# A gated linear-attention layer and its GEGLU block: first-unit PSUM copies on VectorE, constant matmuls in the ramp, and the residual added on VectorE in place of an accumulating DMA

## The chip, the core and the metric

One core of a Trainium2 chip runs the kernel. The metric is device time in microseconds (us) of one execution. The engines are TensorE (PE; its weight loads are PEld), VectorE (DVE), ScalarE (ACT), GpSimd (POOL) and SyncE (SP). SP and POOL issue the DMAs. Each engine takes its instructions in the order in which the compiler laid them down, and waits on semaphores for the others.

## What is computed

The reference has two parts. The first is a recurrence over 768 steps for 4 batches and 8 heads of width 48, with a complex decay per step and channel:

```
mag = sqrt(a_re^2 + a_im^2); scale = min(mag, 0.999) / (mag + 1e-6)
S[t] = (scale * (a_re + i a_im))[t] * S[t-1] + k[t] v[t]^T      (S complex, 48 x 48)
y[t] = q[t] . Re S[t]
```

The second takes x, the 3072 x 384 array of all y, through a gated block and adds x:

```
out = x + sigmoid(x @ w_res) * ((gelu(x @ w_gate) * (x @ w_val)) @ w_out)
```

Inputs and output are float32; d_ff is 1536.

## The kernel before, in words

**Tiling.** The 3072 tokens are cut into 12 groups (g0 to g11) of 256 tokens, two chunks (c = 0, 1) of 128 each; three groups make a batch. The groups are bundled in seven units: [0], [1,2], [3,4], ..., [9,10], [11]. The recurrence is done as chunked attention: the logarithm and the angle of the decay are summed along a chunk by matmuls with triangular matrices; exp and sin/cos of the sums scale q and k, and masked products of the two with v give y; a state per head goes from group to group.

**Two kinds of stage alternate.** `phase_x(u)` is the short one. It holds the output projection of unit u-1 (`op_step`, L459 to L472), the second half of unit u's attention, the decays of unit u+1 (`cs_l`, `carry`, `cs_t`, `p2_sin`) and the first steps of the decays of unit u+2 (`p1_steps`, `p1_arctan`). `phase_y(u)` is the long one: the gate and value matmuls of unit u (`gv_step`, `gp` and `vp`), the products `qE`, `Q`, `kE`, `K` of unit u+1 (`products`), and the first half of its attention. `weave` gives every list of steps a begin and an end as fractions of the stage and sorts all steps by them; the framework then schedules the instructions of each engine, with the attention marked as high priority. ACT changes its function table between stages (L477), and `tab` holds the order of the ACT functions fixed.

**Names that recur.** L124 is the line of all ACT functions that go through `act`: `ar` (Ln and arctan work in place on `ar` and `ai`), `s`, `E` and `Ei` (exp of the sums), `CS` (sine and cosine), `h` (gelu), `sg` (tanh). On DVE: `ai` L189 (the ratio of the decay's parts), `ar` L197 and L198 (log of the size, and its limit), `r` L243, `fg` L244 and `fg` L246 (the angle's fraction, and its absolute value for the cosine), `Q` and `K` L321, `atm` L359 (the mask), `h` L446, `ot` L466. On PE: `csl` L212 and `cst` L236, L238 (the sums, float32), `tp` L346 and L349 (transposes of Q and K), `at` L356, `dk` L386 (the state), `y` L394 and L396, `tpx` L424 (transposes of x), `gp` L439, `vp` L443, `rp` L455, `op` L463.

**Copies out of PSUM in attention.** In each half-head group `grp` the transposed Q goes to SBUF on ACT (L351) and the transposed K on DVE (L352). `x` leaves PSUM on ACT (L399). `xT` leaves it on ACT for even chunks (L428) and on DVE for odd ones (L430). PSUM is fully given out: four buffers for `csl`, `cst`, `ms`, `tpx`, `gp`, `vp`, `rp` and `op` in turn (psM), and one each for `tp`, `at`, `y` and `dk`.

**Residual.** For all units but the last, `ot` is stored by an SP DMA (L470), and a POOL DMA then adds the bfloat16 `x` to the stored rows in memory (L472, `accum_op`). It waits for the store. For the last unit DVE adds `x` to `ot` (L469) before the store. POOL also issues the loads of `v` and of the weights, and the small transfers through DRAM (`dm`, `m`, L262 and L265) that turn a row of decays into a column; DVE multiplies these in `M` L282 and L283.

**The ramp.** In the first stages, before unit 0 has its gate matmuls, the first group's decays, its attention and the decays of g1 to g4 follow each other with little beside them; the loads are in flight at the same time. The stage `phase_x(0)` has its own `weave` (L545 to L549).

Of the kernel before, what the change touches and what calls it, by code (L numbers as in the profile page):

```python
# [28 lines left out]
def kernel(  # L29
# [173 lines left out]
        act(out=T["th", g], in_=T["th", g], func=AF.Arctan)  # L203


    def cs_l(g, c):
        if c == 0:
            T["E", g] = pE.tile([128, W], FP, tag="E", name="E")
            T["Ei", g] = pE.tile([128, W], FP, tag="Ei", name="Ei")
        sl = slice(c * DM, (c + 1) * DM)  # L210
        cs = psM.tile([128, DM], FP, tag="mm", padded_shape=[128, 512], name="csl")
        nc.tensor.matmul(out=cs, lhsT=lmat[c], rhs=T["lm", g][:, sl], start=True, stop=True)  # L212

        def ex():
            act(out=T["E", g][:, sl], in_=cs, func=AF.Exp)
            act(out=T["Ei", g][:, sl], in_=cs, func=AF.Exp, scale=-1.0)
        return ex
# [11 lines left out]
    def cs_t(g, c):  # L229
        s = g % NS  # L230
        th = T["th", g]
        if c == 0:
            T["fg", g] = pE.tile([128, C * H, 2, D], FP, tag="fg", name="fg")
        sl = slice(c * DM, (c + 1) * DM)
        cs = psM.tile([128, DM], FP, tag="mm", padded_shape=[128, 512], name="cst")
        nc.tensor.matmul(out=cs, lhsT=tmat[c], rhs=th[:, sl], start=True, stop=(s == 0))  # L236
        if s > 0:
            nc.tensor.matmul(out=cs, lhsT=ones2pi, rhs=T["P", g], start=False, stop=True)  # L238
        cs3 = cs.rearrange("p (h d) -> p h d", h=H)
        fg = T["fg", g]  # L240
        hs = slice(c * H, (c + 1) * H)
        r = pS.tile([128, H, D], FP, tag="r", name="r")
        nc.vector.tensor_scalar(out=r, in0=cs3, scalar1=MAGIC, scalar2=MAGIC, op0=OP.add, op1=OP.subtract)  # L243
        nc.vector.tensor_tensor(out=fg[:, hs, 1, :], in0=cs3, in1=r, op=OP.subtract)  # L244
        if c == C - 1:
            nc.vector.tensor_scalar(out=fg[:, :, 0, :].bitcast(mybir.dt.int32), in0=fg[:, :, 1, :].bitcast(mybir.dt.int32),  # L246
                                    scalar1=0x7FFFFFFF, scalar2=None, op0=OP.bitwise_and)

    def p2_sin(g):
        T["CS", g] = pQ.tile([128, C * H, 2, D], BF, tag="CS", name="CS")  # L250
# [76 lines left out]
    def attention(g, c):  # L327
        s = g % NS
        first = s == 0 and c == 0
        st = {}  # L330

        def Q(x):
            return T["Q", g][:, x].rearrange("p u d -> p (u d)")

        def K(x):
            return T["K", g][:, x].rearrange("p u d -> p (u d)")

        def V(h):
            return T["v", g][:, c, h]

        def grp(hg):
            def a():
                tp = psT.tile([128, 1024], BF, tag="tp", name="tp")
                for j in range(4):
                    x = c * H + hg * 4 + j
                    nc.tensor.transpose(out=tp[0:DD, j * 128:j * 128 + 128], in_=Q(x), identity=ident)  # L346
                for j in range(4):
                    x = c * H + hg * 4 + j
                    nc.tensor.transpose(out=tp[0:DD, 512 + j * 128:640 + j * 128], in_=K(x), identity=ident)  # L349
                qk = sqp.tile([128, 1024], BF, tag="qk", name="qk")  # L350
                nc.scalar.copy(out=qk[0:DD, 0:512], in_=tp[0:DD, 0:512])  # L351
                nc.vector.tensor_copy(out=qk[0:DD, 512:1024], in_=tp[0:DD, 512:1024])  # L352
                st["qk", hg] = qk
                at = psA.tile([128, 4, 128], FP, tag="at", name="at")
                for j in range(4):
                    nc.tensor.matmul(out=at[:, j], lhsT=qk[0:DD, 512 + j * 128:640 + j * 128],  # L356
                                     rhs=qk[0:DD, j * 128:j * 128 + 128], start=True, stop=True)
                atm = sqp.tile([128, 4, 128], BF, tag="atm", name="atm")
                nc.vector.tensor_tensor(out=atm, in0=at, in1=mask4, op=OP.mult)  # L359
                st["atm", hg] = atm  # L360
            return a

        def enter():
            if s == 0 or c > 0:
                return
            d = T["dk", g - 1][0:DD].rearrange("p (h d) -> p h d", h=H)
            Mb = T["M", g][0:DD].rearrange("p (h u) -> p h u", u=1).to_broadcast([DD, H, D])
            G = stt.tile([128, H, D], FP, tag="G", name="G")
            if s == 1:
                nc.vector.tensor_tensor(out=G[0:DD], in0=d, in1=Mb, op=OP.mult)  # L370
            else:
                nc.vector.tensor_tensor(out=G[0:DD], in0=d, in1=T["G"][0:DD], op=OP.add)
                nc.vector.tensor_tensor(out=G[0:DD], in0=G[0:DD], in1=Mb, op=OP.mult)
            Gb = stt.tile([128, H, D], BF, tag="Gb", name="Gb")
            nc.vector.tensor_copy(out=Gb[0:DD], in_=G[0:DD])
            T["G"] = G
            T["Gbf"] = Gb

        def dk():
            if s == NS - 1 and c == C - 1:  # L380
                return
            if c == 0:
                T["dk", g] = psD.tile([128, DM], FP, tag="dk", padded_shape=[128, 512], name="dk")
            d = T["dk", g]
            for h in range(H):
                nc.tensor.matmul(out=d[0:DD, h * D:(h + 1) * D], lhsT=K(c * H + h), rhs=V(h),  # L386
                                 start=(c == 0 and h == 0), stop=(h == H - 1), skip_group_check=True)

        def yy():
            y = psY.tile([128, DM], FP, tag="y", padded_shape=[128, 512], name="y")  # L390
            for h in range(H):
                ys = y[:, h * D:(h + 1) * D]
                hg, j = divmod(h, 4)
                nc.tensor.matmul(out=ys, lhsT=st["atm", hg][:, j], rhs=V(h), start=True, stop=first)  # L394
                if not first:
                    nc.tensor.matmul(out=ys, lhsT=st["qk", hg][0:DD, j * 128:j * 128 + 128],  # L396
                                     rhs=T["Gbf"][0:DD, h], start=False, stop=True)
            x = xp.tile([128, DM], BF, tag="x", name="x")
            nc.scalar.copy(out=x, in_=y)  # L399
            T["x", g * C + c] = x  # L400
            if c == 0:
                d = T["dk", g][0:DD].rearrange("p (h d) -> p h d", h=H)
                Gb = stt.tile([128, H, D], BF, tag="Gb", name="Gb")
                if s == 0:
                    nc.vector.tensor_copy(out=Gb[0:DD], in_=d)
                else:
                    nc.vector.tensor_tensor(out=Gb[0:DD], in0=d, in1=T["G"][0:DD], op=OP.add)
                T["Gbf"] = Gb

        def hi(f):  # L410
            def w():
                with tc.high_priority():
                    f()
            return w
        return [hi(f) for f in (enter, grp(0), dk, grp(1), yy)]


    def xt_step(u, jj):
# [5 lines left out]
            nc.tensor.transpose(out=tpx[:, f * 128:(f + 1) * 128], in_=x[:, f * 128:(f + 1) * 128], identity=ident)  # L424
        dst = T["xT", u][:, :, jj * 128:(jj + 1) * 128]
        src = tpx.rearrange("p (f t) -> p f t", f=KD)
        if jj % 2 == 0:
            nc.scalar.copy(out=dst, in_=src)  # L428
        else:
            nc.vector.tensor_copy(out=dst, in_=src)  # L430
# [28 lines left out]
    def op_step(u, jj):  # L459
        h2 = T["h2", u]  # L460
        ps = psM.tile([128, DM], FP, tag="mm", padded_shape=[128, 512], name="op")
        for ffi in range(KF):
            nc.tensor.matmul(out=ps, lhsT=h2[:, ffi, jj * 128:(jj + 1) * 128], rhs=wo[:, ffi, :],  # L463
                             start=(ffi == 0), stop=(ffi == KF - 1))
        ot = ob.tile([128, DM], FP, tag="ot", name="ot")
        nc.vector.scalar_tensor_tensor(out=ot, in0=T["sg", u][:, jj], scalar=1.0, in1=ps, op0=OP.add, op1=OP.mult)  # L466
        t0 = token(u, jj) * 128
        if u == NU - 1:
            nc.vector.tensor_tensor(out=ot, in0=ot, in1=T["x", token(u, jj)], op=OP.add)  # L469
        nc.sync.dma_start(out=out[t0:t0 + 128, :], in_=ot)  # L470
        if u < NU - 1:
            nc.gpsimd.dma_start(out=out[t0:t0 + 128, :], in_=T["x", token(u, jj)], accum_op=OP.add)  # L472


    def table(nm):
# [32 lines left out]
    def phase_x(u):  # L508
# [34 lines left out]
        if u == 0:  # L543
            sm = [[call(sums, g) for g in gg if g % NS > 0] for gg in (g1, g2)]
            weave((0.0, 0.25, zip_steps([p1(g) for g in g1])), (0.26, 0.3, csls), (0.31, 0.32, sm[0]), (0.35, 0.45, exs),  # L545
                  (0.4, 0.64, zip_steps([p1(g) for g in g2])), (0.641, 0.642, dec3), (0.645, 0.65, atn[:1]),
                  (0.65, 0.66, [call(p1_arctan, g) for g in g1]), (0.67, 0.85, cst), (0.75, 0.8, atn[1:]),
                  (0.9, 0.95, sin), (0.96, 0.97, sm[1]), (0.0, 0.5, att))
            return  # L549
        if u == 1:  # L550
# [80 lines left out]
```

## Time and profile before

| | |
|---|---|
| median of 3 runs | 324.42 us (323.83 to 324.49) |
| the profiled execution | 324.49 us, span 322.4 us |
| mean granted TensorE clock | 0.949 |
| PE busy | 272.1 us (84%) in 2200 matmuls |
| DVE busy | 234.8 us (73%) in 431 instructions |
| ACT busy | 209.8 us (65%) in 353 |
| POOL busy | 80.5 us (25%) in 115 |
| 22 accumulating DMAs, POOL's part | 20.4 us |
| the chain that ended last | PE 56%, SP's queue 12%, ACT 11%, DMA 9%, DVE 6% |

The span runs from the first to the last instruction of the profiled execution. The shares of busy time are means over stages of different kinds, so they don't say what a change in one stage is worth. The granted clock is given as a share of full speed; a PE that waits is also "busy" in a pipelined matmul, so its share is an upper bound. The chain is followed back from the last instruction, at each step to what released it.

### The profile page before, as it was taken

How to read it: one execution, taken by the hardware profiler on the slowest of the kernel's cores; microseconds unless marked ns; L12 is line 12 of the kernel's file. 1: busy time of each engine (PE TensorE's matmuls, PEld its weight loads, DVE VectorE, ACT ScalarE, POOL GpSimd, SP SyncE). 2: the span in 40 equal slices, each digit the busy share in tenths (PEclk: the TensorE clock that was granted, in tenths of full speed). 3: DMA queues.
4: the chain of work that ended last, by engine and by line, in shares of the span. 5: the costliest groups of instructions: out<-in, count | busy, mean ns of one | idle time of the engine just before them, and what ended most of it. 6: DMA issues, size and time to landing. Idle time of an engine off the chain costs nothing.

```text
span 322.4 us, 5853 instructions
## 1 busy us (share of the span) xinstructions
PE 272.1 (84%) x2200; PEld 170.5 (53%) x2200; DVE 234.8 (73%) x431; ACT 209.8 (65%) x353; POOL 80.5 (25%) x115
## 2 busy tenths in 40 slices
PE   0337927789887999789997999998999999899994
PEld 0116624677543666445664556554656655555682
DVE  2446769968499995599982999974899837864352
ACT  4549684646998557977568976569665683656150
POOL 1206522022040370259020572000630003200220
PEclk9995676959999999999999999999999999999998
DMA  8999999989999995396850595000360003600441
GB/s 159 218 183 181 182 169 165 185 174 180 187 179 186 223 160 33 76 197 113 122 36 2 107 121 95 2 0 3 75 122 3 2 0 76 122 2 0 107 91 50
DMA packets 137755, 34.55 MB, mean 107 GB/s; under 512 B 126848, under 2 KB 137728, under 8 KB 137728
## 3 DMA queue, kind: packets, MB, share of 16 engines
q1 hardware_dynamic: 103296, 23.60, 36.8%
q0 software_dynamic: 34432, 10.59, 31.2%
q8 instruction: 17, 0.28, 0.3%
q14 instruction: 10, 0.08, 0.1%
HBM read 31.31 MB, written 9.07 MB: 125 GB/s over the span
## 4 chain that ended last, share of the span: by engine, by line
PE 56%; SPq 12%; ACT 11%; DMA 9%; DVE 6%; issue 3%; POOL 1%; ACTq 0%; DVEq 0%; POOLq 0%
PE vp L443 14%; PE gp L439 13%; SPq L136 6%; SPq L144 6%; PE op L463 6%; DMA k<-in_k_dram 4%; PE rp L455 3%; PE tp L349 3%; PE tp L346 3%; PE at L356 3%; ACT L477 3%; DMA m<-dm 3%; ACT s L124 3%; PE cst L236 2%; PE y L394 2%
## 5 line engine op out<-in xcount | busy, mean ns | idle before, releaser
L124 ACT ACTIVATE h<-gp 128x512 bf16<-128x512 f32 (+1 forms) x84 | 44.5, 536 | 38.4 <-PE gp L439 37.9
L439 PE MATMUL gp<-xT,wg 128*128 128x512 bf16 (+1 forms) x252 | 65.4, 353 | 3.4 <-ACT h L124 2.0
L443 PE MATMUL vp<-xT,wv 128*128 128x512 bf16 (+1 forms) x252 | 66.6, 353 | 0.0
L446 DVE SCALAR_TENSOR_TENSOR h<-h,vp 128x512 bf16<-128x512 bf16 (+1 forms) x84 | 49.8, 603 | 16.4 <-PE vp L443 12.0
L463 PE MATMUL op<-wo,h 128*128 128x384 bf16 x288 | 50.2, 326 | 8.1 <-ACT Ei L124 5.9
L463 PEld LDWEIGHTS <-h 128*128 128x128 bf16 x288 | 27.8, 98 | 28.7 <-issue 11.3
L351 ACT COPY qk<-tp 96x512 bf16<-96x512 bf16 x48 | 27.9, 580 | 17.1 <-PE tp L349 7.9
L359 DVE TENSOR_TENSOR atm<-at,mask 128x512 bf16<-128x512 f32 x48 | 32.9, 686 | 8.2 <-PE at L356 7.8
L472 POOL DMA_DIRECT2D out_dram<-x x22 | 20.4, 947 | 54.4 <-DMA out_dram<-ot 43.1
L439 PEld LDWEIGHTS <-wg 128*128 128x128 bf16 x252 | 23.7, 99 | 17.9 <-issue 4.2
L443 PEld LDWEIGHTS <-wv 128*128 128x128 bf16 x252 | 23.8, 99 | 13.3
L189 DVE TENSOR_TENSOR ai<-s,ai 128x768 f32<-128x768 f32 x12 | 11.1, 955 | 23.6 <-ACT s L124 23.6
L477 ACT ACT_TABLE_LOAD x21 | 26.9, 1283 | 1.1 <-PEq L615 0.7
L346 PE MATMUL tp<-ident,Q 128*96 128x128 bf16 x192 | 20.1, 231 | 6.9 <-DVE Q L321 6.2
L346 PEld LDWEIGHTS <-Q 128*96 128x96 bf16 x192 | 17.4, 130 | 15.3 <-DVE Q L321 10.0
L124 ACT ACTIVATE CS<-fg,hpi 128x768 bf16<-128x768 f32 x12 | 11.2, 935 | 20.8 <-DVE fg L246 20.7
L150 POOL DMA_DIRECT2D v<-in_v_dram x24 | 21.9, 932 | 4.2 <-DMA v<-in_v_dram 1.3
L349 PE MATMUL tp<-ident,K 128*96 128x128 bf16 x192 | 22.3, 235 | 0.0
L236 PE MATMUL cst<-ai,lt0b 128*128 128x384 f32 x24 | 11.8, 577 | 11.7 <-ACT ai L124 11.0
L352 DVE COPY qk<-tp 96x512 bf16<-96x512 bf16 x48 | 19.8, 413 | 2.3 <-ACT qk L351 1.7
L212 PE MATMUL csl<-ar,lt0a 128*128 128x384 f32 x24 | 11.4, 562 | 10.8 <-DMA ar<-in_a_re_dram 10.8
L466 DVE SCALAR_TENSOR_TENSOR ot<-sg,op 128x384 f32<-128x384 f32 x24 | 13.1, 547 | 10.1 <-PE op L463 10.1
(85 smaller groups left out, 522.0 us busy)
## 6 DMA issues: line engine op xcount, KB each, us to landing
ar<-in_a_re_dram SPq DMA_DIRECT2D x24, 192.0 KB, 4.7
ai<-in_a_im_dram SPq DMA_DIRECT2D x24, 192.0 KB, 4.1
q<-in_q_dram SPq DMA_DIRECT2D x24, 192.0 KB, 3.8
k<-in_k_dram SPq DMA_DIRECT2D x24, 192.0 KB, 3.7
out_dram<-ot SPq DMA_DIRECT2D x24, 192.0 KB, 2.5
out_dram<-x POOLq DMA_DIRECT2D x22, 192.0 KB, 3.7
v<-in_v_dram POOLq DMA_DIRECT2D x24, 96.0 KB, 5.0
wg<-in_moe_w_gate_dram POOLq DMA_DIRECT2D x4, 288.0 KB, 11.4
```

The lines of the kernel that those rows point to most:

```text
L124: tab(nc.scalar.activation(**kw))
L150: nc.gpsimd.dma_start(out=t[:, c], in_=rows(v, g, c))
L346: nc.tensor.transpose(out=tp[0:DD, j * 128:j * 128 + 128], in_=Q(x), identity=ident)
L349: nc.tensor.transpose(out=tp[0:DD, 512 + j * 128:640 + j * 128], in_=K(x), identity=ident)
L351: nc.scalar.copy(out=qk[0:DD, 0:512], in_=tp[0:DD, 0:512])
L359: nc.vector.tensor_tensor(out=atm, in0=at, in1=mask4, op=OP.mult)
L439: nc.tensor.matmul(out=gp, lhsT=wg[:, fi, ffi * 128:(ffi + 1) * 128], rhs=xT[:, fi, :], start=(fi == 0), stop=(fi == KD - 1))
L443: nc.tensor.matmul(out=vp, lhsT=wv[:, fi, ffi * 128:(ffi + 1) * 128], rhs=xT[:, fi, :], start=(fi == 0), stop=(fi == KD - 1))
L446: nc.vector.scalar_tensor_tensor(out=h2[:, ffi, :], in0=h2[:, ffi, :], scalar=0.5, in1=vp, op0=OP.mult, op1=OP.mult)
L463: nc.tensor.matmul(out=ps, lhsT=h2[:, ffi, jj * 128:(jj + 1) * 128], rhs=wo[:, ffi, :], start=(ffi == 0), stop=(ffi == KF - 1))
L472: nc.gpsimd.dma_start(out=out[t0:t0 + 128, :], in_=T["x", token(u, jj)], accum_op=OP.add)
L477: tab(nc.scalar.preload_act_table_set(nm))
```

## The change

There are six edits.

1. `warm(out, n)` is new: n matmuls of constant operands (the identity and the mask) into a PSUM tile that the real matmuls overwrite afterwards. It is called ahead of the first `csl` (10), of the first `cst` of g0 (12) and of g1 (16), of each `at` of g0 (2, four times) and of each `y` of g0 (2, twice).
2. For g0, the copies `qk` (L351) and `x` (L399) go to DVE.
3. For unit 0, both `xT` copies go to DVE (in the kernel before, one of the two).
4. The absolute value in `fg` is made from -f and f by a maximum, in float32, and no longer by a mask on the bits.
5. The arctans of g3 and g4 in `phase_x(0)` move from 0.75-0.8 to 0.98-0.99 of the stage, behind the sines.
6. The residual is added by DVE for every unit, before the store; the accumulating DMA is gone.

```diff
+    def warm(out, n):
+
+        for _ in range(n):
+            nc.tensor.matmul(out=out, lhsT=ident, rhs=mask4.rearrange("p j t -> p (j t)")[:, 0:out.shape[1]],
+                             start=True, stop=True)
+
...
         cs = psM.tile([128, DM], FP, tag="mm", padded_shape=[128, 512], name="csl")
+        if g <= FIRST and c == 0:
+            warm(cs, 10)
...
         cs = psM.tile([128, DM], FP, tag="mm", padded_shape=[128, 512], name="cst")
+        if g <= FIRST + 1 and c == 0:
+            warm(cs, 12 if g <= FIRST else 16)
...
-            nc.vector.tensor_scalar(out=fg[:, :, 0, :].bitcast(mybir.dt.int32), in0=fg[:, :, 1, :].bitcast(mybir.dt.int32),
-                                    scalar1=0x7FFFFFFF, scalar2=None, op0=OP.bitwise_and)
+            nc.vector.scalar_tensor_tensor(out=fg[:, :, 0, :], in0=fg[:, :, 1, :], scalar=-1.0, in1=fg[:, :, 1, :],
+                                           op0=OP.mult, op1=OP.max)
...
-                nc.scalar.copy(out=qk[0:DD, 0:512], in_=tp[0:DD, 0:512])
+                (nc.vector.tensor_copy if g <= FIRST else nc.scalar.copy)(out=qk[0:DD, 0:512], in_=tp[0:DD, 0:512])
...
+                if g <= FIRST:
+                    warm(at.rearrange("p j t -> p (j t)"), 2)
...
+            if g <= FIRST:
+                warm(y, 2)
...
-            nc.scalar.copy(out=x, in_=y)
+            (nc.vector.tensor_copy if g <= FIRST else nc.scalar.copy)(out=x, in_=y)
...
-        if jj % 2 == 0:
+        if jj % 2 == 0 and u > 0:
             nc.scalar.copy(out=dst, in_=src)
...
+        nc.vector.tensor_tensor(out=ot, in0=ot, in1=T["x", token(u, jj)], op=OP.add)
         t0 = token(u, jj) * 128
-        if u == NU - 1:
-            nc.vector.tensor_tensor(out=ot, in0=ot, in1=T["x", token(u, jj)], op=OP.add)
         nc.sync.dma_start(out=out[t0:t0 + 128, :], in_=ot)
-        if u < NU - 1:
-            nc.gpsimd.dma_start(out=out[t0:t0 + 128, :], in_=T["x", token(u, jj)], accum_op=OP.add)
...
-                  (0.65, 0.66, [call(p1_arctan, g) for g in g1]), (0.67, 0.85, cst), (0.75, 0.8, atn[1:]),
+                  (0.65, 0.66, [call(p1_arctan, g) for g in g1]), (0.67, 0.85, cst), (0.98, 0.99, atn[1:]),
```

## The prediction, made before the changed kernel was run

> **What bounds the kernel now.** I read the page's slices first, for the granted clock, then the stages one by one. (Line numbers are those of the kernel before; g0 to g11 are the groups.)
>
> ```profile
> PEclk9995676959999999999999999999999999999998
> ```
>
> A slice is 8.1 us. TensorE runs at reduced clock only between 24 and 72 us: the ramp, from the first unit's attention to the second unit's. Next, busy time by stage; the columns are length, PE, PEld, DVE, ACT, POOL (each with its instructions), granted clock, DMA share and GB/s.
>
> ```profile
> 24.00:38.00 14.00, 10.80 (x88) 8.71 (x89) 10.38 (x17) 10.85 (x18) 8.43 (x11) 0.53 1.16 186
> 44.50:54.20 9.70, 3.96 (x6) 2.14 (x7) 8.02 (x14) 7.68 (x11) 2.77 (x4) 0.50 1.31 179
> 64.80:71.20 6.40, 5.75 (x44) 4.79 (x44) 4.12 (x10) 2.61 (x7) 1.23 (x3) 0.50 0.84 164
> ```
> ```profile
> 173.00:192.00 19.00, 16.54 (x80) 9.22 (x78) 13.68 (x27) 16.57 (x27) 10.05 (x15) 1.00 0.52 80
> 192.00:219.00 27.00, 26.87 (x275) 16.40 (x275) 23.96 (x44) 17.32 (x32) 2.47 (x3) 1.00 0.25 40
> ```
>
> The last two rows are one period of the steady part. The long stage (192 to 219) is bound by PE: busy 26.87 of 27. In the short stage (173 to 192), where the decays of the next unit are made, PE has 2.5 us of idle time. Its DVE looks lightly loaded, but in the timeline it waits 5.1 us for ACT's squares first; from 177.59 to the end it has work without a gap, except one:
>
> ```profile
> DVE M L282 <- DMA m<-dm: 0.7, 1, 0.7
> ```
>
> So each short stage ends through DVE's queue: the second `fg` L246, then ACT's sines and gelu table, then `h`, or L246, then `Q` L321 and the transposes. Work put on DVE between `ai` L189 and `Q` there moves the start of the long stage. That holds in five stages: 83 to 102, 127 to 148, 173 to 192, 219 to 236, 262 to 276. Durations (the last three columns are count, busy us, mean ns, then idle before):
>
> ```profile
> L359 DVE TENSOR_TENSOR atm<-at,mask 128x512 bf16<-128x512 f32 x48 | 32.9, 686 | 8.2 <-PE at L356 7.8
> L352 DVE COPY qk<-tp 96x512 bf16<-96x512 bf16 x48 | 19.8, 413 | 2.3 <-ACT qk L351 1.7
> L197 DVE SCALAR_TENSOR_TENSOR ar<-s,ar 128x768 f32<-128x768 f32 x12 | 11.3, 951 | 3.3 <-ACT s L124 3.3
> L246 DVE TENSOR_SCALAR fg<-fg 128x768 int32<-128x768 int32 x12 | 6.7, 558 | 0.0
> L469 DVE TENSOR_TENSOR ot<-ot,x 128x384 f32<-128x384 f32 x2 | 1.1, 558 | 0.1
> ```
>
> **Residual add.** 22 accumulating DMAs leave the POOL queue (L472, 947 ns each); 22 adds like L469 enter DVE. Back to back, start to start, DVE spends 0.47 us on an operation of this shape (`ot` at 139.94, the next at 140.41), so 10.3 us in all. SP's store waits for the add, and the loads queued behind it on SP start 0.5 us later; DMA share is 0.15 to 0.6 there, so I cost this at nothing. `x` comes free earlier. On POOL the decay transfers `m<-dm` no longer stand behind an accumulation: at most the three waits for `m` (0.7, 1.0, 1.6 us) go, and they cover adds instead.
>
> **fg.** The and-mask (558 ns) becomes a two-operand form; nearest row L197, same shape, 951 ns. So 0.4 us dearer, twelve times, always between `cst` and the sine.
>
> **The five short stages.** I laid the compiled DVE order of the new kernel on the start-to-start times of the old.
> Stage at 83: before the second L246 come one new add, the second `ot` (formerly behind it, 0.47) and two dearer L246 (0.8): L246 ends 1.66 late, `h` and `Q` 1.7.
> Stage at 127: two adds and 0.8, less an operation that moved: `h` 1.5, `Q` 1.1 late; PE had no slack at 148. Taken 1.3.
> Stage at 173: three adds, an `ot` and 0.8, less two `M` operations and their 0.7 wait: `h` 1.2, `Q` 2.3. Taken 1.5.
> Stage at 219: `kE` moves behind the wait for `m` (1.0), which hides it: `h` 0.45, `Q` 1.4. Taken 0.8.
> Stage at 262: the 1.6 wait hides two adds; one dearer L246: 0.4.
> Sum 5.7 us. Bounds: nothing, if PE's idle time (2 to 3 us a stage) takes it all; 10.3 + 4.7 = 15 with every added operation on the path. In the last stage the adds lie beside PE (DVE waits 1.3 to 1.5 us for each `op` there): nothing.
>
> **Ramp, start.** PE gets 14 constant matmuls ahead of the first `csl`. They need the masks (DVE, until 8.23). At half clock a 384-column matmul takes 0.32 us (three of 256 take 0.64 at 67.1), at full clock 0.163 (twelve take 1.95): 4.7 us at half, so they end at about 12.9, where `csl` began at 10.81. `csl` and `cst` then ran at half speed (1.44 from one group to the next); at full speed they take 0.65. `E` of the second half comes 0.7 late if the clock has risen, 1.9 if not; a fast `cst` gives 0.7 back; the dearer L246 takes 0.4. By the first of two rows on the rise (next paragraph) it comes 3.9 us after 8.2, ahead of `csl`. Taken: `Q` +0.3 (bounds -0.4 and +2.3).
>
> The rows for the clock's rise: work resumes at 50.24, and full clock stands from 54.15, 3.9 us later; but between 24 and 37, 77% busy, it did not rise for 13 us. [...]
>
> **Ramp, first attention.** ACT loses four `qk` (580 ns), two `x` (479) and one `xT` (479); DVE takes them at 413 (L352), 548 (L405, a PSUM cast) and 348 (L430). It is ACT that has room: it waits on PE in 31 to 42. DVE is a queue, and the compiled order puts `ar` L197, L198 of g1 behind three, and of g2 behind all four, groups of the first unit's attention. From the first copy (26.7) to the end of L198 of g2 it has eight copies (3.3), four `atm` (2.7), two `x` (1.1), `xT`, `Gb`, two `ai`, two L197, two L198, one `two`: 13.8 us by durations, about 13 start to start, so not before 39.5, where it was 36.55. And it waits for PE: a group is eight transposes, four `at`, four or eight `y`, and now two constant matmuls: 0.86 + 0.43 + 0.33 + 0.85 = 2.5 us at half clock, 1.3 at full. Walking the groups one after the other, L198 of g2 ends at 39.5 with full clock all the way, 42.9 with half, 41.4 if the clock rises at 34.5 (after 30.2 PE is busy without a break, and 4 us are as at 50.24 to 54.15). Then two `csl` halves (0.65 each), two pairs of `E`, `Ei` and the two Ln of g3, g4 on ACT: the last Ln starts at 44.7 against 42.05. ACT is the chain from there to the arctan (7.3 us in both). Taken: +2.65, including the +0.3 (bounds +0.75 and +3.9).
>
> **Ramp, arctan to gelu.** The sixteen constant matmuls follow the last `tpx` (about 44.5) and end by 47 to 49, the arctan at 52.9. What the gap does is in the trace: PE's last matmul before was at 42.4, then
>
> ```profile
> 43.00:44.00 1.00, 0.00 (x0) 0.00 (x0) 1.00 (x2) 1.00 (x2) 0.13 (x1) 1.00 1.49 172
> 44.00:45.00 1.00, 0.00 (x0) 0.00 (x0) 1.00 (x2) 0.71 (x2) 0.00 (x0) 0.53 1.31 193
> ```
>
> So `cst` probably meets half clock again. The rest: a `P` and the first `Q`, `K` leave the space ahead of the second L246 (gain), two L246 are dearer (0.8), the arctans of g3 and g4 (1.5 us) now run between the sines and `qk`, under the wait for `K`'s transposes. Taken -0.5 (bounds -1.3 with full clock, 0). What is late next is the gelu table, as before.
>
> **Sum.** 2.65 - 0.5 + 5.7 = +7.85 us on the profiled execution's 324.49 (span 322.4 and 2.1 around it; the median of three, 324.42, is the same within 0.1). That is 332.3.
>
> **Rivals.**
> 1. The short stages absorb the adds. For: PE idles 2.5 us in 173 to 192, and waits for `m` go. Against: DVE has no other gap. Short stages +1.5 in all, ramp +2.15: 328.1. Chance 0.22.
> 2. Faster: the clock stays full from 24.6 to 71. Place: the three half-clock stretches, with some 9.9 + 3.96 + 5.75 = 19.6 us of PE work, at most 9.8 us back. It decides once more than the 5.7 us of the short stages come back, that is from 60% of it on the path. For: 14 to 18 of the dummies lie in that stretch, and PE's queue is then dense. Against: PE idles from 19 to 24.6, longer than the 2.1 us after which it fell at 44.5, and DVE's queue stays. At its best 324.49 + 5.7 - 9.8 = 320.4; halfway 322.5. Chance 0.10.
> 3. The dummies do nothing to the clock and half speed lasts through the first attention and `cst` (+3.9, 0), with the later of `h` and `Q` deciding in the short stages (1.7 + 1.5 + 2.3 + 1.4 + 0.4 = 7.3): 335.7. Chance 0.18.
> 4. The forecast, 330 to 334: 0.45. The remaining 0.05 is a near draw, 324 to 326.
>
> Range 325.5 to 337: it leaves out the faster case, part of the draw and the far tail of rival 3. A measurement of this kernel tells 0.2% (0.65 us) from no change; faster 0.10, within 0.03, slower 0.87.
>
> **What would show it.** Right: DVE busy about 18 to 20 us more; ACT's first Ln of g3 later by 2 to 4 us; in each short stage the second L246 later by 0.4 to 1.7 us after `ai`; L246 near 950 ns; idle PE ahead of `h` grown. Wrong: granted clock full in 24 to 34, or at `cst` of g1; short stages of unchanged length; an add that costs well under 0.47 us.

## The result, and the profile after

The changed kernel takes **328.79 us** (median of 4 runs, 328.39 to 330.24) against 324.46 us for the kernel before (4 runs); the ratio is 1.0143, with a 95% interval of 1.0106 to 1.018. It is slower, as forecast; of the forecast +7.85 us, 4.3 came in the medians and 4.9 in the spans of the two profiled executions. The profiled execution took 329.15 us, its span 327.3 (before 324.49 and 322.4).

| profiled execution | before | after |
|---|---|---|
| DVE busy, instructions | 234.8 us, 431 | 251.6 us, 460 |
| POOL busy | 80.5 us | 57.7 us |
| ACT busy | 209.8 us | 205.3 us |
| PE busy, matmuls | 272.1 us, 2200 | 279.1 us, 2250 |
| written to memory | 9.07 MB | 4.74 MB |
| mean granted clock | 0.949 | 0.969 |

(The clock's record reads full until its first change, at 23.6 us before and 23.8 after, also where matmuls already ran at half speed: in the kernel before the first `csl` pairs, from 10.81 us on, start 1.44 us apart, and `cst` pairs of the same shape at full clock 0.64; see the last section. So the two mean clocks can't be compared closely.) The page's row of the granted clock, in slices of 8.2 us:

```profile
PEclk9995996979999999999999999999999999999999
```

Where before there were five low slices, four of them in a row, there are now three single ones. Cut to the stretches at half clock (columns as in the prediction, the granted clock fourth from the end, ahead of the DMA share and the rate):

```profile
23.00:34.00 11.00, 7.85 (x67) 6.32 (x68) 7.87 (x15) 8.19 (x10) 7.13 (x10) 0.53 1.16 192
51.00:58.00 7.00, 5.88 (x10) 3.19 (x11) 5.43 (x10) 1.79 (x3) 0.94 (x2) 0.51 1.51 154
68.00:72.00 4.00, 4.00 (x40) 3.37 (x39) 3.20 (x7) 1.86 (x5) 1.93 (x3) 0.57 1.08 216
```

By the clock's record, the time at half clock in them is 10.2, 6.8 and 3.4 us; before it was 13.7, 10.2 and 6.8. One period of the steady part, by the same view:

```profile
176.80:197.60 20.80, 17.66 (x85) 9.88 (x84) 16.18 (x32) 17.14 (x28) 8.42 (x13) 1.00 0.52 77
197.60:224.00 26.40, 25.97 (x272) 16.10 (x271) 23.98 (x43) 16.53 (x32) 0.00 (x0) 1.00 0.04 9
```

The short stage is cut here at ACT's tables (log table to gelu table), so it runs 20.8 us; cut the same way it was 19.6 before. PE has 3.1 us of idle time in it. The groups of DVE instructions (count, busy us, mean ns, idle before):

```profile
L371 DVE TENSOR_TENSOR atm<-at,mask 128x512 bf16<-128x512 f32 x48 | 32.8, 684 | 6.1 <-PE at L368 5.9
L362 DVE COPY qk<-tp 96x512 bf16<-96x512 bf16 x48 | 19.7, 411 | 0.5 <-ACT qk L361 0.3
L481 DVE TENSOR_TENSOR ot<-ot,x 128x384 f32<-128x384 f32 x24 | 13.2, 550 | 0.2
L256 DVE SCALAR_TENSOR_TENSOR fg<-fg 128x768 f32<-128x768 f32 x12 | 11.4, 950 | 0.1
L197 DVE SCALAR_TENSOR_TENSOR ar<-s,ar 128x768 f32<-128x768 f32 x12 | 11.2, 950 | 2.6 <-ACT s L124 2.6
```

The two-operand form of `fg` takes 950 ns, as its neighbour L197, and the 24 adds show 550 ns each. DVE's waits for `m` are down from three (0.7, 1.0 and 1.6 us) to one:

```profile
DVE M L292 <- DMA m<-dm: 0.9, 1, 0.9
```

ACT loads a function table at every change of stage (21 loads of 1.28 us each in both traces), and the starts of those loads cut both spans alike ("log", "arctan" and "gelu table" name the load ahead of those functions):

| stretch | before, us | after, us | change | forecast |
|---|---|---|---|---|
| start to the arctan table (ramp, first attention) | 48.05 | 49.93 | +1.88 | +2.65 |
| arctan table to gelu table of unit 0 | 15.19 | 16.63 | +1.44 | -0.5 |
| first long stage, unit 0 | 20.28 | 18.61 | -1.67 | 0 |
| five short stages | 17.92, 19.18, 19.59, 17.38, 12.04 | 19.32, 20.69, 20.79, 17.45, 12.67 | +1.40, +1.51, +1.20, +0.07, +0.63: +4.8 | +5.7 |
| five long stages behind them, and the tail | 26.40, 25.98, 26.36, 26.32, 23.18, 24.53 | 26.11, 25.55, 26.36, 26.26, 22.73, 24.20 | -1.56 | 0 |
| sum | 322.4 | 327.3 | +4.9 | +7.85 |

### The profile page after: what moved, and what is told of

The parts are those of the page before. It is cut to its first block, busy times and chain, and to the rows that moved or that the text cites. A ratio compares the mean times of both kernels' runs of the same rounds, so it can differ in the third digit from the quotient of the medians.

```text
span 327.3 us, 5927 instructions
## 1 busy us (share of the span) xinstructions
PE 279.1 (85%) x2250; PEld 174.2 (53%) x2250; DVE 251.6 (77%) x460; ACT 205.3 (63%) x346; POOL 57.7 (18%) x93
## 3 DMA queue, kind: packets, MB, share of 16 engines
HBM read 31.31 MB, written 4.74 MB: 110 GB/s over the span
## 5 line engine op out<-in xcount | busy, mean ns | idle before, releaser
L453 PE MATMUL gp<-xT,wg 128*128 128x512 bf16 (+1 forms) x252 | 66.6, 352 | 5.8 <-DVE xT L444 3.5
L124 ACT ACTIVATE h<-gp 128x512 bf16<-128x512 f32 (+1 forms) x84 | 44.5, 536 | 34.0 <-PE gp L453 33.3
L457 PE MATMUL vp<-xT,wv 128*128 128x512 bf16 (+1 forms) x252 | 64.8, 351 | 0.0
L361 ACT COPY qk<-tp 96x512 bf16<-96x512 bf16 x44 | 25.5, 580 | 18.5 <-PE tp L359 11.8
L453 PEld LDWEIGHTS <-wg 128*128 128x128 bf16 x252 | 23.6, 99 | 19.6 <-issue 7.3
L457 PEld LDWEIGHTS <-wv 128*128 128x128 bf16 x252 | 23.8, 98 | 15.2
L124 ACT ACTIVATE CS<-fg,hpi 128x768 bf16<-128x768 f32 x12 | 11.2, 935 | 26.1 <-DVE fg L256 26.1
L356 PEld LDWEIGHTS <-Q 128*96 128x96 bf16 x192 | 16.8, 129 | 16.8 <-DVE Q L331 10.2
L368 PE MATMUL at<-qk 96*128 96x128 bf16 x192 | 19.4, 224 | 0.0
L408 PEld LDWEIGHTS <-atm 128*128 128x128 bf16 x192 | 12.6, 98 | 11.8 <-DVE atm L371 10.6
L124 ACT ACTIVATE E<-csl 128x384 f32<-128x384 f32 x24 | 11.6, 484 | 10.9 <-PE csl L220 10.9
```

Source lines behind the costliest of these rows:

```text
L124: tab(nc.scalar.activation(**kw))
L361: (nc.vector.tensor_copy if g <= FIRST else nc.scalar.copy)(out=qk[0:DD, 0:512], in_=tp[0:DD, 0:512])
L453: nc.tensor.matmul(out=gp, lhsT=wg[:, fi, ffi * 128:(ffi + 1) * 128], rhs=xT[:, fi, :], start=(fi == 0), stop=(fi == KD - 1))
L457: nc.tensor.matmul(out=vp, lhsT=wv[:, fi, ffi * 128:(ffi + 1) * 128], rhs=xT[:, fi, :], start=(fi == 0), stop=(fi == KD - 1))
```

## Experiments

Each ratio is to runs of the kernel before on the same chip, with its 95% interval. Kernels whose names begin with b are the kernel before with one edit; those that begin with a are the changed kernel with one edit undone or altered.

**One edit alone in the kernel before: b_res (the residual), b_fg, b_copy, b_warm.**

```diff
  b_res
-        if u == NU - 1:
+        if True:
             nc.vector.tensor_tensor(out=ot, in0=ot, in1=T["x", token(u, jj)], op=OP.add)
-        if u < NU - 1:
-            nc.gpsimd.dma_start(out=out[t0:t0 + 128, :], in_=T["x", token(u, jj)], accum_op=OP.add)
  b_fg: the lines of fg as in the change
  b_copy: the lines of qk, x and xT as in the change
  b_warm: warm() and its calls as in the change
```

> The kernel before with one edit: the residual is added on VectorE for every unit and the accumulating DMA is gone. Theory (VectorE's queue ends the short stages): the short stages grew by 4.8 us in the changed kernel, of which the dearer L246 explains at most 0.8 in three stages, 0.8 and 0.4 in the others; the adds leave some 2.5 us there and the long stages give up to 1 back: +1 to +3 us. Rival (the adds are covered by waits for m and by PE's idle time, and the cost is in the ramp): within 0.5 us of before, or faster because POOL is freed.

> The kernel before with one edit: the absolute value in fg by a two-operand maximum (0.95 us) and not by the bit mask (0.55 us). Theory: twelve times 0.4 us on VectorE's queue between cst and the sine, each on the path that ends its stage: +2 to +4 us. Rival (hidden behind the sines of the first group, only the second L246 of a stage counts, and less than its 0.4): under +1 us.

> The kernel before with one edit: the first unit's PSUM copies qk, x and xT on VectorE, no constant matmuls. Theory (VectorE is a queue and its first log of g1 and g2 waits behind the first unit's attention): the Ln of g4 starts 1 to 3 us later and the time grows by as much. Rival (ScalarE bounds the ramp, and is relieved of seven copies, 3.8 us): 1 to 3 us faster.

> The kernel before with one edit: the 50 constant matmuls, copies on ScalarE as before. Theory: csl of g0 starts 2 us later and runs at full clock, so E of its second half is 0.5 to 1 late; the clock falls again ahead of the attention and of the second cst; the attention's group is longer by 0.85 us at half clock until the clock rises: between -0.5 and +1.5 us. Rival (the constant matmuls are what the change gains from, and the copies what it loses by): faster by 1 us or more.

Before: 324.07 us, 35 runs. b_res 325.39, ratio 1.0041 [1.0015, 1.0068], about +1.3, as its theory had it. b_fg 326.05, 1.0038 [1.0005, 1.0072], +1.2 by the ratio and +2.0 by the medians, where 2 to 4 were expected; its runs lie between 323.4 and 327.6. b_copy 324.72, 1.0021 [0.9992, 1.0049]: +0.7, not told from nothing, so neither its theory nor its rival. b_warm 323.98, 0.9996 [0.9969, 1.0023]: nothing, so the constant matmuls alone, as the change places them, buy no time.

**One edit undone in the changed kernel: a_acc (the accumulating DMA again), a_and (the mask on the bits again), a_nowarm (no constant matmuls).** Their diffs are the matching parts of the change, reversed.

> The changed kernel with one edit undone: the residual goes back to the accumulating DMA. The single edits on the kernel before add up to +3.1 us (+1.3 adds, +1.2 fg, +0.7 copies, -0.1 constant matmuls) where the whole change costs 4.3 to 4.7. Theory (the adds stand in VectorE's queue ahead of the sine and of Q, and meet there the dearer L246): 2 to 3 us back, the short stages shorter by 2 to 3 us. Rival (the adds are covered, the price of the lone edit came from other orders): under 1 us back.

> The changed kernel with one edit undone: the bit mask in fg is back. Theory (0.4 us for each second L246 on the path, 0.8 where both stand ahead of the sine): 1 to 2.5 us back, most of it in the ramp and in the stages at 95, 141 and 187. Rival (the lone edit's cost was one of a changed order): under 0.7 back.

> The changed kernel without the 50 constant matmuls. Theory (they raise the clock ahead of the first csl, but it falls before the attention and before the second cst, and in the attention VectorE's queue is the bound): the same within 1 us, csl and cst of g0 at half clock again. Rival (they hold the clock in the attention, where it rose at 34 us): 1 to 3 us slower than the changed kernel, with the clock's rise after 36.

Before: 323.77 us, 17 runs. a_acc 325.95, 1.0062 [1.0044, 1.0081]: the residual is worth 2.6 of the 4.6 us that 1.43% is. a_and 326.76, 1.0101 [1.0079, 1.0123]: 1.4. a_nowarm 329.71, 1.0192 [1.0164, 1.0221]: 1.6 *slower* than with the matmuls. Each of these differences is one between two ratios and carries about 1.4 us by their intervals: the 2.6 is clear of nothing, the other two barely or not.

The rival's signs came for a_nowarm: it is slower, and the clock rose at 41.4 us, not at 34.0. But the trace doesn't put the loss there. By ACT's tables a_nowarm is level with the changed kernel behind the ramp and the first long stage (log table at 85.13 against 85.17; it is 1.4 us quicker from the arctan to the gelu table and 1.3 slower in the stage behind it) and still at the next gelu table (104.45 against 104.49). The whole 1.5 us by which its span is longer (328.8 against 327.3) comes in the long stage behind that: 27.60 us against 26.11. What happened in that stage is shown below, under a_long. So in these two traces the constant matmuls buy no time inside the change either.

**Only the constant matmuls ahead of the second `cst`, and as many as fill the wait: b_warm_long.**

```diff
         cs = psM.tile([128, DM], FP, tag="mm", padded_shape=[128, 512], name="cst")
+        if g == FIRST + 1 and c == 0:
+            warm(cs, 44)
```

> The kernel before with constant matmuls in one place only, 44 in the place of the second cst's sixteen: 7.2 us of work at full clock, which is the whole of PE's wait for the arctan. Theory (the sixteen failed since they end 4 to 5 us before they are needed): cst of g1 runs at full clock, the stretch from the arctan's table to the gelu's table, 15.2 us before, is 0.7 to 1.5 shorter, and the time 0 to 1.5 us. Rival (VectorE, not the clock, sets that stretch): its length unchanged within 0.3.

321.67 us, **0.9934** [0.9911, 0.9958]: 2.1 us faster than the kernel before. PE's instructions there (start, us, line, operation, count), which begin at half clock (the record reads 0.50 from 43 to 48 us) and end at full (1.00 from 55 to 66 us, and every pair of `cst` from the first takes 0.81 us):

```profile
43.80 10.13 PE L209 MATMUL cst<-mask,ident 128*128 128x384 bf16 x44
53.77 0.81 PE L244 MATMUL cst<-ai,lt0b 128*128 128x384 f32 x2
```

`cst` starts at once behind the last of them and takes 0.81 us, where it took 1.65 before. The stretch from the arctan table to the gelu table falls from 15.19 to 14.13 us, though the matmuls end later than `cst` could have begun (in the kernel before it begins 2.2 us behind the table's load, here 4.2). The first long stage is 0.60 us shorter as well (19.68 against 20.28), with 3.4 us at half clock in place of 6.8.

The trace does not show the whole 2.1 us. The profiled execution is the slowest of the twelve (324.19 us), and its span is only 0.3 us under that of the kernel before: the arctan table comes 1.5 us later (49.56 against 48.05), ahead of the edit, though ACT and DVE run the same instructions in the same order up to there in both. So 1.5 us in the ramp can differ between two executions of the same code. In this execution `csl` ran at half speed until 39.3 us (the pair at 38.56 still took 1.22 us, that at 39.62 took 0.81), in the other until 37.2 (1.26 us at 36.34, 0.86 at 37.86).

**The three edits of DVE's copies undone (a_nocopy), the arctan put back (a_arct), and more filler in the kernel before (b_hold).**

```diff
  a_nocopy: qk, x and xT on ACT again
  a_arct
-                  ... (0.98, 0.99, atn[1:]),
+                  ... (0.75, 0.8, atn[1:]),
  b_hold: as b_warm_long, and in cs_t, behind the second half's matmul:
+        if g == FIRST and c == 1:
+            hold = psA.tile([128, 4, 128], FP, tag="at", name="hold").rearrange("p j t -> p (j t)")[:, 0:DM]
+            for _ in range(5):
+                nc.tensor.matmul(out=hold, lhsT=tmat[c], rhs=th[:, sl], start=True, stop=True)
```

> The changed kernel with one edit undone: qk, x and xT of the first unit are copied on ScalarE again. Undone singly, the adds gave 2.6 us back and fg 1.4, and the loss of the constant matmuls cost 1.6 more, which leaves some 2.2 of the 4.6 us to the copies and the place of the arctans. Theory (VectorE's logs of g1 and g2 wait behind the attention): the first Ln of g4 earlier by 1 to 2 us and 1 to 2 us back. Rival (it is the place of the arctans, 1.5 us between the sines and qk): under 0.5 back.

> The changed kernel with one edit undone: the arctans of g3 and g4 at their former place. Theory (they stand on the path now: in the changed kernel ScalarE runs them from 64.52 to 65.98, the copy of qk waits for them and the gelu table for the copy): 0.5 to 1.5 us back, the stretch from the arctan's table to the gelu's, 16.6 us, shorter by as much. Rival (K's transposes end no earlier, so qk would wait anyway): within 0.4.

> The kernel before with 44 constant matmuls ahead of the second cst, which alone was 2.1 us faster, and five float32 matmuls of the first group's angles behind the first cst, whose result nothing reads; they can't be moved ahead of the arctan and fill PE's wait of 4.5 us for the first Q. Theory (the attention of the first unit is longer at half clock; TensorE must be kept at work up to its start): full clock from 24 to 37, csl of g1 1 to 2.5 us earlier, the time 0.5 to 2 us under that of the 44 alone. Rival (in that stretch VectorE and ScalarE set the pace): the same as the 44 alone within 0.5.

Before: 324.03 us, 13 runs. a_nocopy 328.29, 1.0145 [1.011, 1.0181]: by the ratio nothing comes back, with some 1.7 us of uncertainty, so the 1 to 2 us of the theory are not seen, nor quite excluded. Its profiled execution is 1.6 us shorter than that of the changed kernel, but only 0.7 of this lies ahead of the arctan table, where the theory puts it; 1.1 lies between the arctan and the gelu table, where `cst` met full clock at first (1.00 until 52.3 us, with PE at work again from 51.44) and 3.4 us of half clock in place of 6.8. a_arct 330.74, 1.021 [1.0182, 1.0238]: putting the arctans back costs 2.2 us more, so that theory fell. In its trace the stretch to the gelu table is shorter, by 0.24 us; the loss lies where the clock was at half for 3.4 us more, in the first long stage (20.31 us against 18.61) and in the long stage looked at under a_long (27.68 against 26.11). b_hold 321.89, 0.9929 [0.9904, 0.9953], the same as b_warm_long: the five float32 matmuls brought full clock for a while only.

```profile
23.00:27.00 4.00, 1.72 (x21) 1.07 (x20) 2.42 (x4) 3.97 (x6) 0.00 (x0) 1.00 1.13 224
27.00:40.50 13.50, 10.95 (x82) 8.09 (x82) 10.35 (x16) 9.08 (x16) 9.10 (x13) 0.50 1.27 180
```

In these rows of b_hold the clock stands at 1.00 to 27 us (and the first four transposes of Q, at 24.62, take 0.42 us, where in the kernel before, at 24.30, they take 0.66); PE was busy for 1.72 of the last 4 us, and then the half-speed stretch comes as long as before (13.6 us of it), only later.

**The changed kernel with 44 in place of 16: a_long.**

```diff
-            warm(cs, 12 if g <= FIRST else 16)
+            warm(cs, 12 if g <= FIRST else 44)
```

> The changed kernel with one number altered: 44 constant matmuls, in place of 16, ahead of the first cst of g1. In the changed kernel the sixteen ended at about 47.7, PE then waited 4.39 us, the clock fell at about 51 and cst, from 52.12, ran at half speed; the stretch from the arctan table to the gelu table took 16.63 us (15.19 in the kernel before). Theory: that half-clock stretch is a good part of what went wrong there. Forty-four reach to about 52.5, cst runs at full clock, the stretch falls to about 15.5 (as 44 of them in the kernel before took it from 15.19 to 14.13), and the time falls by 1 to 2 us against the changed kernel, to 1.008 to 1.012 of the kernel before. Rival: the stretch is set by VectorE's queue (the P operations ahead of r, and the dearer absolute value) whatever the clock: it stays above 16.2 us, and the time stays at 1.013 to 1.016.

Before: 324.19 us, 11 runs. a_long 328.76 (6 runs), 1.0145 [1.0101, 1.0189]: in time, the rival's outcome. The trace says why, and it is neither theory. First PE at the second `cst`:

```profile
44.65 7.31 PE L209 MATMUL cst<-mask,ident 128*128 128x384 bf16 x44
51.81 0.91 PE L246 MATMUL cst<-ai,lt0b 128*128 128x384 f32 x2
```

`cst` runs at full clock and the half-clock stretch at 51 is gone. The stretch to the gelu table falls from 16.63 to 16.12 only, but the first long stage shrinks as well, and by ACT's next two tables (83.50 and 102.82, against 85.17 and 104.49) a_long leads by 1.67 us. Then it loses 1.56 of that in one long stage: 27.67 us against 26.11. PE there, in a_long:

```profile
102.49 0.42 PE L356 MATMUL tp<-ident,Q 128*96 128x128 bf16 x4 [0.38 <-DVE Q L331]
104.76 0.95 PE L453 MATMUL gp<-xT,wg 128*128 128x512 bf16 x3 [1.85 <-ACT h L124]
```
```profile
104.00:104.50 0.50, 0.00 (x0) 0.00 (x0) 0.50 (x2) 0.49 (x2) 0.00 (x0) 1.00 1.20 244
104.50:105.00 0.50, 0.24 (x2) 0.12 (x2) 0.50 (x2) 0.50 (x2) 0.00 (x0) 1.00 1.02 201
105.00:105.50 0.50, 0.50 (x3) 0.19 (x2) 0.50 (x2) 0.20 (x1) 0.00 (x0) 0.79 1.25 257
105.50:106.00 0.50, 0.50 (x7) 0.49 (x6) 0.50 (x2) 0.25 (x1) 0.00 (x0) 0.50 1.32 345
```

The value in brackets is PE's idle time ahead of the instruction: 1.85 us, for the first gelu `h`. Half a microsecond behind it, at 105.29 us, the granted clock falls to 0.50, for 3.4 us, in the stage that PE bounds (busy for 25.3 of 26.4 us in the kernel before). In the changed kernel the same wait is there, and the clock did not fall in the profiled run:

```profile
106.43 0.81 PE L453 MATMUL gp<-xT,wg 128*128 128x512 bf16 x3 [1.85 <-ACT h L124]
```

In the kernel before the wait is shorter:

```profile
103.38 0.81 PE L439 MATMUL gp<-xT,wg 128*128 128x512 bf16 x3 [1.10 <-ACT h L124]
```

All fourteen traces sort by this one wait and by where it fell. In each trace the changes of the granted clock lie on one grid with a step of 3.41 us: in a_long at 23.37, 33.61, 64.33, 71.16, 105.29 and 108.70 us. The grid lies differently from trace to trace (carried back to the span's start, its first line is at 0.5 us in a_nowarm, 1.7 in b_warm_long and 3.3 in the changed kernel). I cut the stage along the grid of its own trace:

| wait of PE for the first `h` of that stage | kernels | longest part of it in one step of the grid | PE busy in that step | clock fell | length of the long stage |
|---|---|---|---|---|---|
| 1.10 to 1.42 us | before, b_fg, b_copy, b_warm, b_warm_long, b_hold, a_acc | 1.42 us or less | 1.99 us or more | in none of 7 | 26.4 to 26.5 us |
| 1.85 to 1.86 us | after, a_and, a_nocopy | 1.09, 1.13, 1.34 us | 1.94, 2.28, 2.07 us | no | 26.0 to 26.1 us |
| 1.85 us | b_res, a_nowarm, a_arct, a_long | 1.85, 1.73, 1.85, 1.85 us | 1.57, 1.30, 1.18, 1.18 us | yes, 3.4 us of half clock | 27.6 to 27.7 us |

The rows of one step each, first the changed kernel (its wait runs from 104.58 to 106.43, and the grid cuts it at 105.67), then a_long (102.91 to 104.76, whole in one step), each with the step behind it:

```profile
102.26:105.67 3.41, 1.94 (x12) 0.79 (x10) 3.41 (x5) 2.85 (x3) 0.18 (x1) 1.00 1.10 239
105.67:109.09 3.42, 2.66 (x25) 1.64 (x25) 3.40 (x7) 2.30 (x5) 0.00 (x0) 1.00 1.05 231
```
```profile
101.88:105.29 3.41, 1.18 (x9) 0.60 (x8) 3.41 (x5) 3.29 (x5) 0.00 (x0) 1.00 1.06 234
105.29:108.70 3.41, 3.41 (x20) 1.84 (x19) 2.56 (x6) 1.18 (x2) 0.00 (x0) 0.50 0.92 204
```

The seven kernels with the long wait are just those in which DVE adds the residual. In this stage the add therefore had a second price in four of their traces: about 1.6 us, in those where 1.73 us or more of the 1.85 fell into one step. In the changed kernel, a_and and a_nocopy the grid cut the wait, and no more than 1.34 us fell into one. I take that for the luck of one execution: the runs without a trace can't be sorted so. It fits that five runs of a_arct have a mean clock of 0.958 or 0.959 and take 330.2 to 331.5 us, and one has 0.969 and takes 329.6: 0.010 of 328 us is 3.3 us of clock, which is 6.6 us at half clock, or two steps. In which stages those lay is not shown. Nor does PE's busy time in a step sort other stages: in the kernel before PE was busy for 2.02 us from 61.14 to 64.55 and the clock fell, and for 1.63 us from 173.78 to 177.19 and it did not.

## Why the prediction was right, and where it was not

Direction and range were right; the sum was 3.0 us too large by the profiled spans and 3.5 by the medians. The median lies below the forecast's own band of 330 to 334 us. It is closest to rival 1 (328.1), but not for its reason: the short stages did not absorb the adds. The misses by term are -0.8, +1.9, -1.7, -0.9 and -1.6 us in the order of the table, so that the fit within the ramp and the first long stage is partly luck: two misses of nearly 2 us cancel there.

**Ramp, start: right.** The constant matmuls ran from 8.18 to 12.83 us (forecast 8.2 to 12.9); the clock rose, by the times of the matmuls, before the second half of `csl`, which took 0.81 us where it had taken 1.49.

**Ramp, first attention: near in size, +1.88 for +2.65, but its mechanism is not shown.** L198 of g2 ended at 40.69 us (forecast 41.4, before 36.55), the clock rose at 34.0 (34.5), and the last Ln came 1.87 us later. The mis-sized term is the walk through DVE's queue: it ended 0.7 us earlier than I had it. Its reading as the price of the *copies* is not borne out: in time a_nocopy gives nothing back. The later Ln is a fact of the trace, but undoing the copies brought the arctan table forward by 0.7 us only. And +1.88 is no more than this stretch differs without any edit in it: to the arctan table it takes 48.05, 47.65 and 49.56 us in the kernel before, b_res and b_warm_long, whose ACT and DVE run the same instructions in the same order up to there. One trace for each kernel can't tell the price of the copies from that.

**Ramp, arctan to gelu: wrong, +1.44 for -0.5.** That `cst` would meet half clock was right. PE in the kernel before, then in the changed kernel:

```profile
50.24 1.65 PE L236 MATMUL cst<-ai,lt0b 128*128 128x384 f32 x2 [7.84 <-ACT ai L124]
```
```profile
44.96 2.76 PE L209 MATMUL cst<-mask,ident 128*128 128x384 bf16 x16
52.12 1.65 PE L246 MATMUL cst<-ai,lt0b 128*128 128x384 f32 x2 [4.39 <-ACT ai L124]
```

The sixteen ended at 47.7, the clock fell at about 51, and `cst` began at 1.65 us a pair. The step that failed is "the arctans of g3 and g4 now run between the sines and `qk`, under the wait for `K`'s transposes". ACT, in the kernel before and in the changed kernel:

```profile
61.83 0.83 ACT L124 ACTIVATE CS<-fg 128x768 bf16<-128x768 f32 x1
62.65 0.58 ACT L351 COPY qk<-tp 96x512 bf16<-96x512 bf16 x1
63.24 1.28 ACT L477 ACT_TABLE_LOAD   x1
```
```profile
62.94 0.94 ACT L124 ACTIVATE CS<-fg,hpi 128x768 bf16<-128x768 f32 x1 [1.45 <-DVE fg L256]
63.78 0.83 ACT L124 ACTIVATE CS<-fg 128x768 bf16<-128x768 f32 x1
64.52 1.56 ACT L124 ACTIVATE ai<-ai 128x768 f32<-128x768 f32 x2
65.98 0.56 ACT L361 COPY qk<-tp 96x512 bf16<-96x512 bf16 x1
66.56 1.28 ACT L488 ACT_TABLE_LOAD   x1
```

There is no gap: the two arctans stand on ACT's path, sine to `qk` to table. From the start of `cst` to what follows the sines on ACT the stretch has not changed (12.40 us against 12.41); I take it that what left DVE's queue there, the dearer L256 and the later rise of the clock cancel. The arctans, 1.46 us from start to start, are the whole difference between these two traces. In the old order they ran under `cst`. Yet undoing the move is no gain: in a_arct the table is only 0.24 us nearer (16.39), since `P` and `Q` are back ahead of the second L256, and the half-clock stretch behind it is 6.8 us instead of 3.4. So the move costs what the trace shows, and what it gives back elsewhere is not settled; in the kernel before it was not tried alone. (The clock fell at 44.1 us in the row that the prediction shows, 1.7 us after PE's last matmul; it read 44.5 and 2.1.)

**First long stage of unit 0: a term that was missing, -1.67.** I had taken the half-clock stretch at 64.8 to 71.2 as unchanged. It shrank from 6.8 to 3.4 us in a stage in which PE is busy for 19.3 of 20.3 us. a_nowarm shows what this is worth: it has the same 227 matmuls in that stage and 6.8 us of half clock, and the stage takes 19.94 us against 18.61, so 1.3 of the 1.67. Rival 2 had the mechanism and asked for too much of it.

**Short stages: right, +4.8 for +5.7.** The adds and L256 stand in DVE's queue where the prediction had them, ahead of the second L256 (L246 in the kernel before, shown first):

```profile
189.39 0.55 DVE L244 TENSOR_TENSOR fg<-cst,r 128x384 f32<-128x384 f32 x1
189.86 0.54 DVE L466 SCALAR_TENSOR_TENSOR ot<-sg,op 128x384 f32<-128x384 f32 x1
190.32 0.55 DVE L246 TENSOR_SCALAR fg<-fg 128x768 int32<-128x768 int32 x1
```
```profile
193.57 0.54 DVE L480 SCALAR_TENSOR_TENSOR ot<-sg,op 128x384 f32<-128x384 f32 x1
194.04 0.54 DVE L254 TENSOR_TENSOR fg<-cst,r 128x384 f32<-128x384 f32 x1
194.50 0.54 DVE L481 TENSOR_TENSOR ot<-ot,x 128x384 f32<-128x384 f32 x1
194.97 0.94 DVE L256 SCALAR_TENSOR_TENSOR fg<-fg 128x768 f32<-128x768 f32 x1
```

An add takes 0.47 us from start to start, as counted. From the start of a stage's last `ai` to the end of its second L246 or L256, DVE takes 10.46, 12.11, 12.40 and 11.91 us in the first four short stages of the kernel before, and 11.86, 13.62, 13.61 and 11.98 in the changed one: longer by 1.40, 1.51, 1.21 and 0.07 us, just as the stages are. So the queue up to the second L256 sets their end. Four stages lie within 0.3 us of the forecast; the stage of 219 gave +0.07 for +0.8, where the wait for `m` probably hid more than I took. The traces of the single edits price the two edits apart:

| profiled execution | ramp and first long stage | five short stages | five long stages and tail | span |
|---|---|---|---|---|
| before | 83.5 | 86.1 | 152.8 | 322.4 |
| b_res | 82.8 | 88.3 | 153.3 | 324.4 |
| b_fg | 85.9 | 88.3 | 150.6 | 324.8 |
| after | 85.2 | 90.9 | 151.2 | 327.3 |
| a_acc | 84.2 | 88.4 | 150.6 | 323.2 |
| a_and | 85.1 | 88.1 | 151.6 | 324.8 |

In the short stages the adds cost 2.2 us alone and the dearer L246 2.2 us; both together 4.8; undone singly they give 2.6 and 2.9 back. The four other kernels that keep both edits (a_nowarm, a_nocopy, a_arct, a_long) have 90.8 to 91.1 us there, b_copy and b_warm 85.2 and 85.7.

**Long stages: a term that was missing, -1.56.** I counted the start of each long stage and took its length as fixed. Where the adds hold a stage back, the next one is shorter (26.11 us against 26.40 behind the first): PE has run more of its matmuls ahead, as I read it, for in that stage it is busy for 24.3 us against 25.3 and has 30 `vp` matmuls left against 33. b_fg gives 1.8 us back in the long stages, of the 2.2 that it loses in the short ones. In the changed kernel 1.2 us come back so, a quarter of the short stages' loss; the other 0.3 are the tail, which is as short (24.2 us) in b_copy and b_warm_long, where neither edit is. The sign that the prediction named for a late stage, idle PE ahead of `h`, did grow, from 1.10 to 1.85 us; DVE's busy time grew by 16.8 us, for 18 to 20 forecast.

**What stays open.** In time the edits do not add up: undone one at a time they give 2.6, 1.4, -1.6, 0 and -2.2 us, 0.2 in sum where the change cost 4.6. In the short stages they do, as the table shows. The rest moves with the clock: a_nowarm's loss and 1.6 us of a_arct's are the fall in one long stage, and the same order of instructions on ACT and DVE took 47.65 to 49.56 us in the ramp. I could not hold the place of the clock's grid fixed, and each kernel has one trace, so how the medians divide into edit and clock is not settled, and the prices of the copies, of the arctans' place and of the constant matmuls in the ramp stay open.

## What to carry to other kernels

Filler matmuls paid where they reached the work that they were to serve: sixteen that ended 4.4 us early met half clock again, 44 that ended at `cst` took 0.66% off the kernel before, and that version beats both kernels (for part of the gain the trace shows the place, 1.1 us at `cst` and 0.6 in the stage behind it). Work moved onto an engine with idle time on average is priced in the stage where its queue sets the end, and part of that price comes back in the next stage if the bounding engine can run ahead (here 4.8 us in the short stages, 1.2 back in the long ones). Where a wait of the bounding engine grows, look at the clock behind it before anything else: with three quarters of a microsecond more of waiting (1.85 us for 1.10) the clock fell in four of seven traces, which cost 1.6 us, twice as much. And where single edits don't add up in time, add them up by stage, each in its own trace.

## What the runs showed of the hardware

The half-clock stretches came in multiples of 3.41 us (3.4, 6.8, 10.2 and 13.7 us, 17.1 in a_nocopy and 23.9 in a_nowarm; only the one at the end of a trace is cut off), and the granted clock read 1.00 or 0.50, between them only in rows that hold a change. One such stretch in a long stage cost 1.6 us, in the first one 1.3.

The clock fell 1.7 us after PE's last matmul ahead of the second `cst` in the kernel before (42.4 to 44.1), and 3.3 us after the last of the sixteen in the changed kernel (47.7 to 51.1). In the long stage looked at under a_long it fell in four of the seven traces with an idle time of 1.85 us, 0.5 to 1.4 us behind the end of that time or, in a_nowarm, 0.1 us ahead of it; PE was busy for 1.18 to 1.57 us in the step that the fall ended.

With PE busy for 7.84 of 10.24 us, from 23.75 to 33.99 in the changed kernel, the clock stayed at half. And the granted clock in the profile reads full before its first recorded change although matmuls ran at half speed: in the kernel before the first change stands at 23.6 us, but `csl` at 10.81 took 1.44 us from one group to the next, and `cst` of the same shape 0.64 at full clock (54.93 to 55.57). So "only between 24 and 72 us" in the prediction is too narrow.
